# Cross network on one core: 32 rows of first-layer remainder weights copied on the chip, and VectorE's remainder copies ahead of three product pairs

## The chip, the cores and the metric

The kernel runs on one core of one Trainium2 chip. The metric is the device time of one execution in microseconds. Below, PE is TensorE (PEld its weight loads), DVE is VectorE, ACT is ScalarE, POOL is GpSimd and SP is SyncE. SP and ACT also issue DMA transfers, each from its own instruction queue.

## What is computed

```python
B, F, D, L = 4096, 26, 16, 6          # Din = F * D = 416
def reference(x0, ws, bs):            # x0 [4096, 416], ws [6, 416, 416], bs [6, 416], all bf16
    x = x0
    for l in range(ws.shape[0]):
        x = x0 * (x @ ws[l] + bs[l]) + x
    return x
```

Six layers; each is one matrix product over 416 features, a bias, a product with `x0` and a sum with the layer's input.

## The kernel before

The activations are held transposed on the chip: features on partitions, batch rows on columns. The 416 features are three full blocks of 128 (`XM`, index m for outputs, k for inputs) and a **remainder** of 32 (`XR`). The 4096 batch columns are two **halves** s = 0, 1 of 2048; a half is four **groups** g of 512 columns, and groups 0, 1 and 2, 3 form the two **pairs** h = 0, 1. The remainder of the four groups of a half lies on the four bands of 32 partitions of one tile, so its weights must be there four times: `WR` holds the 32 remainder rows of the weights on each band of 32 partitions. `XRd` holds `XR[0]` with the bands swapped by 64 partitions, and `WD` a 32-column slice of `WR`, each band in its own block.

The parts of the head that the change touches, by line:

- `load_x0t` (L76): one transposing DMA on SP for each group of a half, from `x0` in memory into `XM[0]`; eight in all. `load_xrem0` (L81): four DMAs on ACT that bring the remainder of half 0 into `xrig`. `load_xrem1` (L85): one DMA on SP that brings the remainder of half 1 into `xrem`; POOL rearranges it into `xrig` (L128).
- `load_wr0` (L88): one DMA on ACT that reads the 32 remainder rows of layer 0 four times, as a broadcast, into the 128 partitions of `WR`. `load_wr` (L91) does the later layers, four DMAs of 32 rows on SP. `fill_wd` (L125) copies from `WR` into `WD` on POOL.
- L106 is a small ACT instruction that makes the activation table load early.
- `first_layer(s)` runs layer 0 for one half. `full` (L206) multiplies the three full blocks of one group, `row` (L213) adds the remainder's part from `WR`, `mm_rem` (L185, L190) makes the remainder's output in `pr`. `x0_rem` transposes `xrig` on PE (L151) and copies the result on DVE into `XR[0]` once and into `XRd` in two parts (L154); for half 1 this stands inside `first_layer(0)`, after `mm_rem`, in the second bank of `pr`.
- `ew_main`: ACT evicts a PSUM tile with the bias (L159), DVE multiplies by `x0` (L160) and adds the layer's input (L161); these two are called a product pair below. `ew_rem` does the same for the remainder (L165, L166, L167).

PE in half 0 goes: the three `full` of group 0, the transposes of `xrig`, the three `full` of group 1, eight row matmuls (four calls of `row`, two matmuls each: three close the tiles of pair 0, one opens the first of pair 1), 18 matmuls of `full` for pair 1 (groups 2 and 3), four row matmuls, `mm_rem`, the transposes for half 1; then half 1 in the same manner. Four PSUM buffers of two banks go round among the tiles; the first tile of pair 1 in half 1, opened by the row matmuls, takes the buffer of half 0's `pr`, so it waits until ACT's L165 has read that.

Within an engine the order is made by a scheduler from the program and its own estimates; an instruction marked with `keep_in_program_order` is not moved past others so marked or ahead of its place. Each DMA signals one of eight completion semaphores, taken in turn; a DMA that takes a semaphore in use waits for the transfer before it.

Of the kernel before, what the change touches and what calls it, by code (L numbers as in the profile page):

```python
# [10 lines left out]
ALU = mybir.AluOpType  # L11
# [5 lines left out]
def kernel(  # L17
# [7 lines left out]
    nc = tc.nc  # L25
    B, D = x0.shape
    L = ws.shape[0]
    P = 128
    NK = 3
    R = D - NK * P  # L30
    assert R == 32 and B == 4096 and D == 416 and L >= 2
    NS = 2
    NG = 4
    CW = 512
# [18 lines left out]
    WR = const.tile([P, L, D], BF16)  # L53
# [11 lines left out]
    XM = [big.tile([P, NK, B], BF16, name=f"XM{i}") for i in range(3)]  # L65
    XR = [big.tile([P, NS * CW], BF16, name=f"XR{i}") for i in range(3)]

    def col0(s, g):
        return SW * s + CW * g
# [4 lines left out]
    def load_x0t(s, g):  # L74
        c0 = col0(s, g)
        nc.sync.dma_start_transpose(out=XM[0][:, :, c0:c0 + CW], in_=x0[c0:c0 + CW, 0:NK * P])  # L76
# [8 lines left out]
            nc.sync.dma_start(xrem[:], x0_v[:, 16:32, NK * P:D])  # L85

    def load_wr0():
        nc.scalar.dma_start(WR[:, 0, :], ws[0:1, NK * P:D, :].broadcast_to([NG, R, D]))  # L88

    def load_wr(eng, g, l0, l1):  # L90
        eng.dma_start(WR[32 * g:32 * g + 32, l0:l1, :], ws[l0:l1, NK * P:D, :].rearrange("l r n -> r l n"))  # L91
# [11 lines left out]
    load_x0t(0, 1)  # L103
    load_xrem0()
    load_wr0()
    nc.scalar.activation(dz[:, 1:2], dz[:, 0:1], ACT.Identity, bias=dz[:, 0:1], scale=1.0)  # L106
    for g in range(2, NG):
        load_x0t(0, g)
    load_x0t(1, 0)
# [39 lines left out]
    def x0_rem(s, tpr):  # L149
        for i in range(4):  # L150
            nc.tensor.transpose(tpr[:, 128 * i:128 * i + 128], xrig[:, s, i, :], ident[:])  # L151
        for dst, src in ((slice(0, P), slice(0, P)), (slice(64, P), slice(0, 64)), (slice(0, 64), slice(64, P))):
            to = XR[0] if dst == src else XRd
            nc.vector.tensor_copy(to[dst, CW * s:CW * s + CW], tpr[src])  # L154

    def ew_main(l, s, m, h, pt, cur, nxt):
        c0 = col0(s, 2 * h)
        t = tpool.tile([P, 2 * CW], BF16, name="t")
        nc.scalar.activation(t[:], pt[:].rearrange("p a b -> p (a b)"), ACT.Identity, bias=bM[:, m, l:l + 1], scale=1.0)  # L159
        nc.vector.tensor_tensor(out=t[:], in0=t[:], in1=XM[0][:, m, c0:c0 + 2 * CW], op=ALU.mult)  # L160
        nc.vector.tensor_tensor(out=nxt[:, m, c0:c0 + 2 * CW], in0=t[:], in1=cur[:, m, c0:c0 + 2 * CW], op=ALU.add)  # L161

    def ew_rem(l, s, pr, curR, nxtR):
        tr = tpool.tile([P, 2 * CW], BF16, name="t")
        nc.scalar.activation(tr[:, 0:CW], pr, ACT.Identity, bias=bR[:, l:l + 1], scale=1.0)  # L165
        nc.vector.tensor_tensor(out=tr[:, 0:CW], in0=tr[:, 0:CW], in1=XR[0][:, CW * s:CW * s + CW], op=ALU.mult)  # L166
        nc.vector.tensor_tensor(out=nxtR[:, CW * s:CW * s + CW], in0=tr[:, 0:CW], in1=curR[:, CW * s:CW * s + CW], op=ALU.add)  # L167
# [15 lines left out]
    def mm_rem(l, s, pr, cur, curR):  # L183
        for g in range(NG):
            nc.tensor.matmul(pr[32 * g:32 * g + 32, :], lhsT=WD[:, l, g, :], rhs=curR[:, CW * s:CW * s + CW],  # L185
                             start=True, stop=False, tile_position=(0, 32 * g))
        for k in range(NK):
            for g in range(NG):
                c0 = col0(s, g)
                nc.tensor.matmul(pr[32 * g:32 * g + 32, :], lhsT=WM[:, l, k, NK * P:D], rhs=cur[:, k, c0:c0 + CW],  # L190
                      start=False, stop=(k == NK - 1), tile_position=(0, 32 * g))
# [8 lines left out]
    def first_layer(s):  # L200
        cur, curR, nxt, nxtR = XM[0], XR[0], XM[1], XR[1]

        def full(pt, m, h, gl, after_row):
            c0 = col0(s, 2 * h + gl)
            for k in range(NK):
                nc.tensor.matmul(pt[:, gl, :], lhsT=WM[:, 0, k, 128 * m:128 * m + 128], rhs=cur[:, k, c0:c0 + CW],  # L206
                                 start=(k == 0 and not after_row), stop=(k == NK - 1 and after_row))

        def row(pt, m, h, opens):
            for gl in range(2):  # L210
                rg = 32 * ((2 * h + gl) ^ (2 if m == 1 else 0))
                src = XRd if m == 1 else curR
                nc.tensor.matmul(pt[:, gl, :], lhsT=WR[rg:rg + 32, 0, 128 * m:128 * m + 128],  # L213
                                 rhs=src[rg:rg + 32, CW * s:CW * s + CW],
                                 start=opens, stop=not opens, tile_position=(rg, 0))

        def ph(m):
            return psum.tile([P, 2, CW], FP32, tag="ps", name=f"ph{m}")

        pa = [ph(m) for m in range(NK)]  # L220
        if s == 0:
            for m in range(NK):
                full(pa[m], m, 0, 0, False)
            tp0 = psum.tile([P, CW], BF16, tag="ps", name="tpr")
            x0_rem(0, tp0[:])
            for m in range(NK):
                full(pa[m], m, 0, 1, False)
        else:
            for m in range(NK):
                for gl in range(2):  # L230
                    full(pa[m], m, 0, gl, False)
        pb = [ph(0)]
        row(pa[0], 0, 0, False)
        row(pb[0], 0, 1, True)
        row(pa[2], 2, 0, False)
        row(pa[1], 1, 0, False)
        for m in range(NK):
            ew_main(0, s, m, 0, pa[m], cur, nxt)
        for m in range(NK):
            if m:  # L240
                pb.append(ph(m))
            for gl in range(2):
                full(pb[m], m, 1, gl, m == 0)
        row(pb[1], 1, 1, False)
        row(pb[2], 2, 1, False)
        pr = psum.tile([P, 2, CW], FP32, tag="ps", name="pr")
        mm_rem(0, s, pr[:, 0, :], cur, curR)
        if s == 0:
            x0_rem(1, pr[:, 1, :].bitcast(BF16)[:, 0:CW])
        for m in range(NK):  # L250
            ew_main(0, s, m, 1, pb[m], cur, nxt)
        ew_rem(0, s, pr[:, 0, :], curR, nxtR)

    bias_setup()
# [1 line left out]
    for s in range(NS):  # L256
        first_layer(s)
# [15 lines left out]
    cur, curR = XM[1], XR[1]  # L273
    for l in range(1, LL):
        nxt, nxtR = XM[1 + (l % 2)], XR[1 + (l % 2)]
# [4 lines left out]
        def finish(t):  # L280
            s, m = t
            for h in range(2):
                ew_main(l, s, m, h, pts[t][h], cur, nxt)
            if feeds_last:
                xl_dmat(s, m, nxt)
# [19 lines left out]
        cur, curR = nxt, nxtR  # L305

    l = LL
# [97 lines left out]
```

## Time and profile before

Device times, 3 runs: median 131.31 us (131.15 to 131.46).

| what | value |
|---|---|
| profiled execution, its own time | 131.51 us |
| span, from first to last instruction | 129.7 us |
| PE busy | 123.4 us, 95% |
| DVE busy | 107.5 us, 83% |
| ACT busy | 85.7 us, 66% |
| POOL busy | 6.1 us, 5% |
| mean granted TensorE clock | 0.992 |
| DMA | 16.45 MB, 42185 packets |

Rows of a timeline are: start in us, length in us, engine, line, operation, written tile <- read tiles, count; in square brackets the engine's idle time before, and what ended it. SPq and ACTq are instructions of a queue, such as the issue of a DMA; the length of such a row is the issue's, and the landing comes later. Rows of groups end in busy time in us, mean ns of one, and idle time before with what ended it. Several instructions merged in a row overlap, since matmuls are pipelined.

### The profile page before, as it was taken

Reading aid. Unit: us, or ns where it says so; the run is one execution under the profiler, and the core shown is the slowest. Engines: PE = TensorE matmul, PEld = TensorE weight load, DVE = VectorE, ACT = ScalarE, POOL = GpSimd, SP = SyncE. Lnnn points to the kernel's source line nnn. Section 1 sums busy time; section 2 is a strip of 40 time slices with the busy share of each in tenths; the row PEclk is TensorE's granted clock in tenths of the full one; section 3 lists DMA queues with packets and bytes.
Section 4 is the critical chain, followed back from the end, with each engine's and each line's share of the span. In section 5 each row is a group of like instructions: output and inputs, shape, how many; then the busy total and the mean of one; then the engine's idle time right before and its main releaser. Section 6 shows DMA issues by size and latency. Waiting matters only on the chain.

```text
span 129.7 us, 3968 instructions
## 1 busy us (share of the span) xinstructions
PE 123.4 (95%) x1690; PEld 55.1 (42%) x1690; DVE 107.5 (83%) x197; ACT 85.7 (66%) x97; POOL 6.1 (5%) x17
## 2 busy tenths in 40 slices
PE   6999999999999999999999999999999999999960
PEld 2333343444444444444444444444444445445430
DVE  1022999999998898999898989898989899888992
ACT  0044865976849486849476849577848896569670
POOL 4002200800000000000000000000000000000000
PEclk9999999999999999999999999999999999999996
DMA  3999999999990000000000000000197989996754
GB/s 91 240 222 226 167 163 269 257 329 333 332 274 7 0 5 3 5 0 5 0 5 0 5 0 5 0 0 5 26 180 163 121 180 199 187 315 195 237 182 137
DMA packets 42185, 16.45 MB, mean 127 GB/s; under 512 B 30894, under 2 KB 42168, under 8 KB 42168
## 3 DMA queue, kind: packets, MB, share of 16 engines
q1 hardware_dynamic: 39368, 15.53, 54.3%
q10 hardware_dynamic: 2800, 0.67, 2.6%
q8 instruction: 13, 0.21, 0.7%
q14 instruction: 4, 0.03, 0.1%
HBM read 6.23 MB, written 3.41 MB: 74 GB/s over the span
## 4 chain that ended last, share of the span: by engine, by line
PE 73%; DVE 11%; DMA 8%; issue 3%; ACT 2%; DVEq 0%; ACTq 0%
PE pt L173 49%; PE py L319 8%; PE pt L179 5%; PE pr L190 4%; DMA WR<-in_ws_dram 4%; DMA XM<-in_x_dram 4%; DVE t L347 3%; PE ph L206 3%; DVE t L160 2%; DVE XM L161 2%; DVE o L336 2%; PE pr L185 2%; PE ph L213 1%; PE py L325 1%; ACT t L159 1%
## 5 line engine op out<-in xcount | busy, mean ns | idle before, releaser
L173 PE MATMUL pt<-XM,WM 128*32 128x512 bf16 x1152 | 65.2, 379 | 0.0
L159 ACT ACTIVATE t<-pt,bM 128x1024 bf16<-128x1024 f32 x48 | 49.6, 1115 | 18.3 <-PE pt L179 18.3
L160 DVE TENSOR_TENSOR t<-t,XM 128x1024 bf16<-128x1024 bf16 x60 | 41.4, 690 | 6.0 <-ACT t L159 6.0
L161 DVE TENSOR_TENSOR XM<-t,XM 128x1024 bf16<-128x1024 bf16 x60 | 41.8, 697 | 3.5
L173 PEld LDWEIGHTS <-WM 128*32 128x32 bf16 x1152 | 29.7, 97 | 33.8 <-issue 5.1
L346 ACT CAST t<-py 128x416 bf16<-128x416 f32 (+1 forms) x23 | 14.8, 642 | 4.8 <-PE py L319 2.1
L319 PE MATMUL py<-WM,XM 128*128 128x416 bf16 x96 | 17.7, 340 | 0.0
L206 PE MATMUL ph<-XM,WM 128*128 128x512 bf16 x72 | 16.5, 379 | 0.2 <-DMA XM<-in_x_dram 0.2
L159 ACT ACTIVATE t<-ph,bM 128x1024 bf16<-128x1024 f32 x12 | 12.5, 1115 | 4.9 <-PE ph L213 4.9
L319 PEld LDWEIGHTS <-XM 128*128 128x128 bf16 x96 | 9.0, 98 | 8.5 <-issue 1.4
L347 DVE TENSOR_TENSOR t<-t,X0rows 128x416 bf16<-128x416 bf16 (+1 forms) x23 | 10.4, 454 | 1.2 <-ACT t L346 1.2
L206 PEld LDWEIGHTS <-WM 128*128 128x128 bf16 x72 | 6.8, 98 | 8.6 <-issue 1.2
L336 DVE TENSOR_TENSOR o<-t,XLrows 128x416 bf16<-128x416 bf16 (+1 forms) x23 | 10.3, 451 | 0.0
L165 ACT ACTIVATE t<-pr,bR 128x512 bf16<-128x512 f32 x10 | 6.4, 684 | 5.0 <-DVE XRd L154 2.9
L190 PE MATMUL pr<-XM,WM 128*32 128x512 bf16 x120 | 8.2, 379 | 0.0
L179 PE MATMUL pt<-XR,WR 32*128 32x512 bf16 x96 | 7.3, 379 | 0.0
L106 ACT ACT_TABLE_LOAD x1 | 1.3, 1283 | 6.4 <-DMA XM<-in_x_dram 6.4
L135 PE MATMUL wps<-warm 128*128 128x512 bf16 (+1 forms) x11 | 4.1, 561 | 1.2 <-DVE warm L94 1.2
L167 DVE TENSOR_TENSOR XR<-t,XR 128x512 bf16<-128x512 bf16 x10 | 4.2, 424 | 0.7
L190 PEld LDWEIGHTS <-WM 128*32 128x32 bf16 x120 | 3.2, 97 | 3.0
L125 POOL COPY WD<-WR 32x32 bf16<-32x32 bf16 (+1 forms) x8 | 3.6, 454 | 16.0 <-DMA WR<-in_ws_dram 15.6
L166 DVE TENSOR_TENSOR t<-t,XR 128x512 bf16<-128x512 bf16 x10 | 4.2, 418 | 0.0
(37 smaller groups left out, 29.6 us busy)
## 6 DMA issues: line engine op xcount, KB each, us to landing
X0rows<-in_x_dram SPq DMA_DIRECT2D x4, 832.0 KB, 11.6
out_dram<-o SPq DMA_DIRECT2D x9, 208.0 KB, 2.6
WM<-in_ws_dram SPq DMA_DIRECT2D x5, 312.0 KB
out_dram<-o SPq DMA_DIRECT2D x13, 104.0 KB, 1.9
WR<-in_ws_dram SPq DMA_DIRECT2D x4, 130.0 KB, 4.2
WM<-in_ws_dram ACTq DMA_DIRECT2D x1, 312.0 KB
XM<-in_x_dram SPq DMA_TRANSPOSE x8, 5.7
xrig<-in_x_dram ACTq DMA_DIRECT2D x4, 32.0 KB, 4.3
```

The lines of the kernel that those rows point to most:

```text
L159: nc.scalar.activation(t[:], pt[:].rearrange("p a b -> p (a b)"), ACT.Identity, bias=bM[:, m, l:l + 1], scale=1.0)
L160: nc.vector.tensor_tensor(out=t[:], in0=t[:], in1=XM[0][:, m, c0:c0 + 2 * CW], op=ALU.mult)
L161: nc.vector.tensor_tensor(out=nxt[:, m, c0:c0 + 2 * CW], in0=t[:], in1=cur[:, m, c0:c0 + 2 * CW], op=ALU.add)
L165: nc.scalar.activation(tr[:, 0:CW], pr, ACT.Identity, bias=bR[:, l:l + 1], scale=1.0)
L173: nc.tensor.matmul(pts[g // 2][32 * q:32 * q + 32, g % 2, :], lhsT=WM[:, l, k, 128 * m + 32 * q:128 * m + 32 * q + 32], rhs=cur[:, k, c0:c ...
L179: nc.tensor.matmul(pts[g // 2][:, g % 2, :], lhsT=WR[32 * g:32 * g + 32, l, 128 * m:128 * m + 128], rhs=curR[32 * g:32 * g + 32, CW * s:CW ...
L190: nc.tensor.matmul(pr[32 * g:32 * g + 32, :], lhsT=WM[:, l, k, NK * P:D], rhs=cur[:, k, c0:c0 + CW], start=False, stop=(k == NK - 1), tile ...
L206: nc.tensor.matmul(pt[:, gl, :], lhsT=WM[:, 0, k, 128 * m:128 * m + 128], rhs=cur[:, k, c0:c0 + CW], start=(k == 0 and not after_row), sto ...
L319: nc.tensor.matmul(py[:, 0:D], lhsT=cur[:, k, q_cols(q, g)], rhs=WM[:, l, k, :], start=((not closes) and k == 0), stop=(closes and k == NK ...
L336: tc.keep_in_program_order(nc.vector.tensor_tensor(out=o, in0=t, in1=xl, op=ALU.add))
L346: nc.scalar.copy(tv, src)
L347: tc.keep_in_program_order(nc.vector.tensor_tensor(out=tv, in0=tv, in1=X0rows[:, b, :], op=ALU.mult))
```

## The change

The load of the first layer's remainder weights is now one DMA of the 32 rows into the first band of `WR`. It is issued on SP, behind the first two groups of `x0` (the scheduler puts it there too: on SP the list begins with two transposes, this load, then the other transposes). Three copies on the chip fill the other bands: two on ACT and one on POOL, behind L106 and ahead of `fill_wd`. And in half 0 the products of pair 1 carry the mark that keeps them in program order, so DVE makes the three copies of `x0_rem` for half 1 ahead of the fourth, fifth and sixth product pair; before, the scheduler had put them behind the fifth. PE's order is the same in both.

```diff
     def load_wr0():
-        nc.scalar.dma_start(WR[:, 0, :], ws[0:1, NK * P:D, :].broadcast_to([NG, R, D]))
+        nc.sync.dma_start(WR[0:R, 0, :], ws[0, NK * P:D, :])
...
     load_wr0()
     nc.scalar.activation(dz[:, 1:2], dz[:, 0:1], ACT.Identity, bias=dz[:, 0:1], scale=1.0)
+    for g in range(1, NG):
+        dst, src = WR[32 * g:32 * g + 32, 0, :], WR[0:R, 0, :]
+        if g < NG - 1:
+            nc.scalar.copy(dst, src)
+        else:
+            nc.gpsimd.tensor_copy(dst, src)
...
-    def ew_main(l, s, m, h, pt, cur, nxt):
+    def ew_main(l, s, m, h, pt, cur, nxt, pin=False):
...
-        nc.vector.tensor_tensor(out=t[:], in0=t[:], in1=XM[0][:, m, c0:c0 + 2 * CW], op=ALU.mult)
+        prod = nc.vector.tensor_tensor(out=t[:], in0=t[:], in1=XM[0][:, m, c0:c0 + 2 * CW], op=ALU.mult)
+        if pin:
+            tc.keep_in_program_order(prod)
...
         for m in range(NK):
-            ew_main(0, s, m, 1, pb[m], cur, nxt)
+            ew_main(0, s, m, 1, pb[m], cur, nxt, pin=(s == 0))
```

## The prediction

> **What bounds the kernel now.** I read the page first, then busy time by stage, then the chain of waits, and last the timelines of PE, DVE and SP over the first 35 us.
>
> ```profile
> 27.50:104.70 77.20, 77.20 (x1381) 34.56 (x1374) 69.99 (x115) 56.02 (x59) 0.00 (x0) 1.00 0.31 69
> ```
>
> A row of the stages: start and end, length, busy time and instructions of PE, PEld, DVE, ACT and POOL, granted clock, DMA share, GB/s. From 27.5 to 104.7 us PE is busy for all of 77.20 us at a granted clock of 1.00, so nothing edited before 27.5 us can shorten that stage; it can only start it earlier. The question is how many microseconds PE loses in the head. The chain of waits (start, length, what) shows two places.
>
> ```profile
> 0.74 5.01 DMA XM<-in_x_dram
> 5.76 5.23 DMA WR<-in_ws_dram
> 11.04 0.41 PE ph L213 x2
> ...
> 19.67 0.42 DVE XR L154
> 20.12 0.42 DVE XRd L154
> 20.56 0.44 DVE XRd L154
> 21.08 0.70 ACT t L165
> 21.82 0.60 PE ph L213 x6
> ```
>
> First, the remainder weights land at 5.76 + 5.23 = 10.99 and release the row matmuls. Second, ACT's eviction L165 stands behind VectorE's copies L154, and PE's rows behind L165, because `pr` gives back a PSUM buffer. PE's timeline gives the sizes.
>
> ```profile
> 8.83 2.10 PE L206 MATMUL ph<-XM,WM 128*128 128x512 bf16 x9
> 11.04 0.60 PE L213 MATMUL ph<-XR,WR 32*128 32x512 bf16 x6
> 11.59 4.15 PE L206 MATMUL ph<-XM,WM 128*128 128x512 bf16 x18
> 15.67 0.39 PE L213 MATMUL ph<-XRd,WR 32*128 32x512 bf16 x2
> 16.97 0.40 PE L151 MATMUL pr<-ident,xrig 128*128 128x128 bf16 x4
> 17.20 4.05 PE L206 MATMUL ph<-XM,WM 128*128 128x512 bf16 x18
> 21.19 0.39 PE L213 MATMUL ph<-XR,WR 32*128 32x512 bf16 x2
> 21.82 0.40 PE L213 MATMUL ph<-XR,WR 32*128 32x512 bf16 x4 [0.24 <-ACT t L165]
> 22.35 4.06 PE L206 MATMUL ph<-XM,WM 128*128 128x512 bf16 x18
> ```
>
> Undisturbed, 18 matmuls of L206 take 21.19 - 17.20 = 3.99 us up to the next rows. One step is (4.05 - 2.10)/9 = 0.217 us, so 9 of them take 3.99 - 9 x 0.217 = 2.04 us. Three losses follow:
> - the first rows could start at 8.83 + 2.04 = 10.87 and start at 11.04: **0.17 us**, waiting for WR;
> - the next 18 take 15.67 - 11.59 = 4.08 instead of 3.99: **0.09 us**. The only input first used there that can be late is the fourth x0 group, read from the fourth matmul on, so I put its landing at about 12.3 us (an estimate, 11.59 + 3 x 0.217 + 0.09);
> - the eight rows of the first half take 11.59 - 11.04 = 0.55 us, those of the second 22.35 - 21.19 = 1.16: **0.61 us**, waiting for L165. Only 0.24 is printed as idle; the rest is the pipe running dry.
>
> **The change, part by part.**
>
> *VectorE order (0.61 us).* In the compiled order nothing moves on PE; on DVE the three copies L154 stand after the third product pair instead of the fifth.
>
> ```profile
> 15.51 0.93 POOL L128 COPY xrig<-xrem 128x512 bf16<-128x512 bf16 x1 [3.39 <-DMA xrem<-in_x_dram]
> 16.01 0.98 DVE L161 TENSOR_TENSOR XM<-t,XM 128x1024 bf16<-128x1024 bf16 x1
> 31.44 0.41 DVE L167 TENSOR_TENSOR XR<-t,XR 128x512 bf16<-128x512 bf16 x1
> 34.42 0.22 PE pr L185 x4
> ```
>
> The third pair ends at 16.01 + 0.98 = 16.99, the transposes L151 that feed the copies at 16.97 + 0.40 = 17.37. With the first rows 0.17 earlier and PE 0.26 earlier, DVE has its pairs done at 16.82 and the transposes at 17.11. The copies wait some 0.3 to 0.4 us at the head of DVE's queue, with the fourth to sixth products behind them. They take 20.56 + 0.44 - 19.67 = 1.33 us and end near 18.5; L165 ends near 19.3, and PE's rows want it at 21.19 - 0.26 = 20.93. So the stall of 0.61 goes, with 1.6 us of cover. What is late next is DVE: it reaches the end of the first layer at 31.85 - 0.17 + 0.4, near 32.1. The first matmuls that need all of that are L185 of the second half, at 34.42, or 33.55 after the whole gain: 1.4 us of cover. Bounds: 0 gained if xrem comes so late that the copies gain nothing, 0.61 at best. I take 0.61.
>
> *WR on SP, 32 rows instead of 128 (0.17 us).* The load leaves ACT's queue, where it was issued after the first x0 group had landed, and stands on SP behind two transposes.
>
> ```profile
> 5.76 0.65 ACTq L88 DMA_DIRECT2D WR<-in_ws_dram  x1
> 2.17 2.69 SPq L76 DMA_TRANSPOSE XM<-in_x_dram  x1
> DMA to landing us min/median/max: 6.6/6.6/6.6
> 4.92 1.90 SPq L76 DMA_TRANSPOSE XM<-in_x_dram  x1
> 6.86 2.19 SPq L76 DMA_TRANSPOSE XM<-in_x_dram  x1
> 11.45 0.59 SPq L85 DMA_DIRECT2D xrem<-in_x_dram  x1
> DMA to landing us min/median/max: 3.9/3.9/3.9
> WR<-in_ws_dram SPq DMA_DIRECT2D x4, 130.0 KB, 4.2
> ```
>
> SP's second transpose ends its issue at 2.17 + 2.69 = 4.86, so WR is issued near 4.92. The landing rows are of that transpose (6.6, so 8.77), of xrem (3.9) and of the later WR loads (4.2). Bounds for its landing: 4.92 + 3.9 = 8.8 below, 10.99 as now above. I take 4.92 + 4.2 = 9.1, just behind the transpose ahead of it. Then two ACT copies and one POOL copy of 32x416, which the trace does not show. The nearest rows:
>
> ```profile
> L270 ACT COPY XLrows<-scrR 128x512 bf16<-128x512 bf16 x2 | 1.2, 625 | 0.7 <-DMA scrR<-XR 0.7
> L106 ACT ACTIVATE dz<-dz 128x1 f32<-128x1 f32 x1 | 0.3, 295 | 0.0
> L128 POOL COPY xrig<-xrem 128x512 bf16<-128x512 bf16 x1 | 0.9, 932 | 3.4 <-DMA xrem<-in_x_dram 3.4
> L125 POOL COPY WD<-WR 32x32 bf16<-32x32 bf16 x4 | 0.8, 204 | 9.2 <-DMA WR<-in_ws_dram 9.0
> ```
>
> ACT: between 295 and 625 ns; by width 0.295 + 415/511 x 0.330 = 0.56 us, two 1.13. POOL: between 204 and 932; by width 0.79. From 9.1 plus 0.1 for the semaphore ACT is done near 10.3, POOL near 10.0; PE wants them at 10.87. ACT has nothing else to do there (its first eviction follows the rows), and POOL's small copies L125 behind the new one are wanted only by L185, near 16 us. So the copies cost nothing while WR lands before 10.87 - 1.23 = 9.64; after that each microsecond costs one. I take the whole 0.17.
>
> *The transposes behind it (0.09 us).* Two effects pull apart. In the compiled order the third transpose now waits for the semaphore of the first, which lands at 5.75 (0.74 + 5.01 in the chain; ACT's old WR issue at 5.76 waited for the same), so its issue moves from 4.92 to about 5.8: **+0.88** for it and all that follows on SP, xrem included, plus the 26 KB. Against that stands a hole in the transfers:
>
> ```profile
> 8.30:9.60 1.30, 1.29 (x7) 0.59 (x7) 0.69 (x2) 0.00 (x0) 0.00 (x0) 1.00 1.26 295
> 9.60:10.70 1.10, 1.10 (x7) 0.39 (x4) 0.58 (x2) 0.00 (x0) 0.00 (x0) 1.00 1.29 101
> 10.70:12.00 1.30, 1.19 (x12) 0.33 (x11) 0.00 (x0) 0.53 (x1) 0.69 (x4) 1.00 1.28 287
> ```
>
> The last column is GB/s: 295, then 101, then 287, with the engines nominally busy throughout. The 1.1 us hole lies at the end of the WR transfer (landing 10.99), so I read it as transposes held up until WR's engines are through: at 290 GB/s it costs 1.1 x (290 - 101)/290 = 0.72 us. If it goes with the broadcast, the fourth group lands at 12.3 + 0.88 - 0.72 = 12.46 where every issue delay counts in full, and at 12.3 - 0.72 = 11.6 where the queue behind the second transpose covers the late issue. The second is nearer: its data still arrive until 8.77, 3 us after the new issue. PE wants that group at 12.34 - 0.09 - 0.17 = 12.08. I take it as in time: 0.09 gained; bounds 0.38 lost with the hole gone, and 1.1 lost with the hole left.
> The Trainium skill, DMA: Bandwidth & Descriptors, Rules for kernel authors, says that a leading zero-stride broadcast of c copies keeps a transfer on at most c engines. By it WR's broadcast of four copies sits on four and the 32-row form on sixteen, the hole goes and the sum below stands; without it rival 4 weighs more. The hole agrees with it but does not prove it.
>
> *Sum.* 0.61 + 0.17 + 0.09 = 0.87 us. The profiled execution took 131.51 us, 0.20 above the median 131.31; 130.64 on its scale, **130.44** against the median. PE's later stages have no gap to take it back, and the tail hangs on PE's end.
>
> **The rivals.**
> 1. *Only the VectorE order pays.* The fourth group still lands at 12.3, and the rows' 0.17 are spent waiting there: 131.31 - 0.61 = 130.70. For: 0.09 is lost there already. Against: the hole.
> 2. *The copies gate the rows.* WR lands 5.23 us after its issue, as now, at 10.15; the copies end at 11.38, 0.51 past 10.87: gain 0.36, 130.95. Against: it is a quarter of the bytes.
> 3. *The copies do not come forward.* xrem, last in the delayed line, holds POOL's copy and PE's transposes; the wait moves from L165 to L151, and only WR's part stays: 131.31 - 0.26 = 131.05. It decides from xrem 0.3 us later than now (POOL ends at 15.51 + 0.93 = 16.44, PE comes at 16.71) and has taken the 0.61 at 0.9 later.
> 4. *Slower: the third and fourth groups come late.* The hole is not the broadcast's, the issue delay counts in full: the fourth lands at 12.3 + 0.88 + 0.1 = 13.28 instead of 12.08, PE waits 1.2 us, and 131.31 - 0.87 + 1.2 = 131.64. It decides from a landing of 12.95. For: the transposes' issue is SP's only work there, back to back. Against: the rate outside the hole shows engines, not issue, as the limit.
>
> 5. *No change: SP's issue time passes on.* WR's own issue, 0.65 us on ACT, is added to SP's line, and the fourth group lands that much later, at 12.95; PE waits 0.87 us, and the time is 131.31. For: SP's issues follow each other without a pause (4.92 + 1.90 = 6.82, then 6.86). Against: the same rate. The Trainium skill, DMA: Bandwidth & Descriptors, Issuing engines are not separate DMA queues, says that a second issuing engine saves only the sequencer's issue time; the move gives that back. Whether it shows here the trace before cannot tell.
>
> **How the numbers follow.** Forecast 0.60, rival 1 0.12, rival 2 0.08, rival 3 0.08, rival 4 0.08, rival 5 0.04. The range runs from 130.2 (the forecast less the runs' scatter of 0.15 and the rounding of the steps) to 131.05, through rival 3; rivals 4 and 5, 0.12, stay outside. About 0.2%, 0.26 us, is what can be told from no change. Faster: forecast and rivals 1 and 2, 0.80; same: rivals 3 (at the edge) and 5, 0.12; slower: rival 4, 0.08.
>
> **What would show it.** The order step is right if L165 of the first half ends before 20 us and the eight rows of the second half take 0.55 us; wrong if L151 or L213 waits there. The WR step is right if WR lands near 9.1 and the first rows start near 10.87 with no wait on ACT or POOL. The transfer step is right if the 1.1 us hole is gone and the 18 matmuls after the first rows take 3.99 us. The forecast fails if PE waits for an x0 group, or if L185 of the next layer starts waiting on DVE.

## The result, and the profile after

The changed kernel takes 130.77 us (median of 13 runs, 130.49 to 131.15), the kernel before, run beside it, 131.28 (13 runs, 131.15 to 131.59): a ratio of 0.9965, 95% interval 0.9956 to 0.9974. The gain is 0.51 us, not the 0.87 of the forecast. The two profiled executions are further apart, 131.51 and 130.71, by 0.80; that contrast is taken up below.

PE's timeline of the changed kernel (the three blocks' matmuls are L214 now, the rows L221):

```profile
8.62 2.10 PE L214 MATMUL ph<-XM,WM 128*128 128x512 bf16 x9
10.66 0.60 PE L221 MATMUL ph<-XR,WR 32*128 32x512 bf16 x6
...
11.20 4.34 PE L214 MATMUL ph<-XM,WM 128*128 128x512 bf16 x18
15.47 0.39 PE L221 MATMUL ph<-XRd,WR 32*128 32x512 bf16 x2
...
21.00 0.60 PE L221 MATMUL ph<-XR,WR 32*128 32x512 bf16 x6
...
21.54 4.06 PE L214 MATMUL ph<-XM,WM 128*128 128x512 bf16 x18
```

The second half's rows take 21.54 - 21.00 = 0.54 us instead of 1.16: that stall is gone. The first rows begin at 10.66, directly behind the nine matmuls before them. But the 18 matmuls after them take 15.47 - 11.20 = 4.27 us, where 3.99 is the undisturbed time: PE loses 0.28 there, not 0. VectorE's timeline around the copies of the remainder:

```profile
17.21 0.42 DVE L160 COPY XR<-pr 128x512 bf16<-128x512 bf16 x1 [0.61 <-PE pr L157]
17.67 0.86 DVE L160 COPY XRd<-pr 64x512 bf16<-64x512 bf16 x2
```

ScalarE's, with the copies of `WR` and the eviction of `pr`:

```profile
8.82 1.10 ACT L110 COPY WR<-WR 32x416 bf16<-32x416 bf16 x2 [2.89 <-DMA WR<-in_ws_dram]
...
18.62 0.69 ACT L173 ACTIVATE t<-pr,bR 128x512 bf16<-128x512 f32 x1 [0.60 <-DVE XRd L160]
```

GpSimd's copy of `WR`:

```profile
8.94 0.53 POOL L112 COPY WR<-WR 32x416 bf16<-32x416 bf16 x1 [6.81 <-DMA WR<-in_ws_dram]
```

The copies of the remainder stand at 17.21 to 18.53, after 0.61 us at the head of DVE's queue, and the eviction of `pr` (L173) is through at 19.31, 1.7 us before PE wants it. WR has landed at 8.82, the copies on the chip end at 9.92 and 9.47, and PE comes at 10.66. The 0.28 us has its row in SP's timeline and in the chain of waits. SP first, then the chain:

```profile
4.77 0.57 SPq L88 DMA_DIRECT2D WR<-in_ws_dram  x1
5.61 5.17 SPq L76 DMA_TRANSPOSE XM<-in_x_dram  x3
```
```profile
0.74 4.86 DMA XM<-in_x_dram
5.61 1.44 SPq L76
7.10 5.00 DMA XM<-in_x_dram
12.14 3.40 PE ph L214 x15
...
126.04 0.29 DVEq L408
```

The first x0 group lands at 0.74 + 4.86 = 5.60; SP, which is done with the issue of `WR` at 4.77 + 0.57 = 5.34, issues the third transpose at 5.61, with the semaphore that this landing gives back (SP's waits put 0.3 us down to it); the fourth goes out at 7.10 and lands at 12.10, and only then do 15 of the 18 matmuls start. The last row stands behind DVE's last result, at 126.04. The stages, with GB/s in the last column:

```profile
8.30:9.60 1.30, 1.22 (x7) 0.60 (x7) 0.91 (x3) 0.75 (x2) 0.61 (x2) 1.00 1.12 237
9.60:10.70 1.10, 1.10 (x10) 0.34 (x11) 0.36 (x1) 0.32 (x1) 0.73 (x4) 1.00 1.24 267
10.70:12.00 1.30, 1.30 (x12) 0.38 (x12) 0.00 (x0) 0.91 (x1) 0.00 (x0) 1.00 1.04 138
...
27.50:104.70 77.20, 77.20 (x1374) 34.50 (x1362) 70.44 (x116) 56.01 (x59) 0.00 (x0) 1.00 0.33 72
```

The hole of 101 GB/s is filled (267), but the stages beside it are lower than before: 237 for 295 GB/s ahead of it, 138 for 287 behind it. From 8.30 to 12.00 us the change moves 781 KB (1.30 x 237 + 1.10 x 267 + 1.30 x 138) where the kernel before moves 868, at most 78 of them for the larger load of `WR` (104 KB instead of 26), so the x0 groups as a whole are no further on at 12 us. The middle of the kernel is as full as before: whatever the head gains is kept.

A second profiled execution of the kernel before, 131.35 us, is nearer to the median; it is called the usual one below. Its PE timeline, and two rows of its chain:

```profile
10.83 0.60 PE L213 MATMUL ph<-XR,WR 32*128 32x512 bf16 x6
...
11.37 4.29 PE L206 MATMUL ph<-XM,WM 128*128 128x512 bf16 x17
15.60 0.39 PE L213 MATMUL ph<-XRd,WR 32*128 32x512 bf16 x2
...
21.12 0.88 PE L213 MATMUL ph<-XR,WR 32*128 32x512 bf16 x6
...
22.14 0.82 PE L206 MATMUL ph<-XM,WM 128*128 128x512 bf16 x3
```
```profile
8.79 2.09 PE ph L206 x9
10.87 0.36 PE ph L213 x2
```

Here the first rows start at 10.83 and the chain goes to them from the nine matmuls before, not from WR; the 18 matmuls take 15.60 - 11.37 = 4.23 (0.24 lost; in the change, and with order only below, the chain puts such a loss down to the fourth x0 group), and the second half's eight rows take 22.14 - 21.12 = 1.02, a stall of 0.48 behind L165. In the execution that the prediction read, with its rows at 11.04, WR came some 0.2 us later than here. The two further profiles with the broadcast, those of order only below, have their first rows at 10.79 and 10.69, directly behind the nine matmuls as well.

### The profile page after: what moved, and what is told of

Its sections match the earlier page's. It is cut to its first block, busy times and chain, and to the rows that moved or that the text cites. A ratio compares the mean times of both kernels' runs of the same rounds, so it can differ in the third digit from the quotient of the medians.

```text
span 128.9 us, 3973 instructions
## 1 busy us (share of the span) xinstructions
PE 123.1 (96%) x1690; PEld 54.9 (43%) x1690; DVE 107.1 (83%) x197; ACT 86.9 (67%) x99; POOL 5.9 (5%) x18
## 4 chain that ended last, share of the span: by engine, by line
PE 80%; DMA 8%; DVE 5%; issue 2%; SPq 1%; ACT 1%; DVEq 0%
PE pt L181 49%; PE ph L214 9%; DMA XM<-in_x_dram 8%; PE py L327 8%; PE pt L187 5%; PE pr L198 5%; DVE t L355 3%; DVE o L344 2%; PE pr L193 2%; SPq L76 1%; PE py L333 1%; PE ph L221 1%; PE py L336 1%; ACT t L354 1%; PE pr L157 0%
## 5 line engine op out<-in xcount | busy, mean ns | idle before, releaser
L165 ACT ACTIVATE t<-pt,bM 128x1024 bf16<-128x1024 f32 x48 | 49.6, 1115 | 18.3 <-PE pt L187 18.3
L214 PE MATMUL ph<-XM,WM 128*128 128x512 bf16 x72 | 16.5, 379 | 0.1
L165 ACT ACTIVATE t<-ph,bM 128x1024 bf16<-128x1024 f32 x12 | 12.5, 1114 | 4.4 <-PE ph L221 4.4
L214 PEld LDWEIGHTS <-WM 128*128 128x128 bf16 x72 | 6.8, 98 | 8.6 <-issue 1.3
L173 ACT ACTIVATE t<-pr,bR 128x512 bf16<-128x512 f32 x10 | 6.4, 684 | 2.7 <-PE pr L198 2.1
L175 DVE TENSOR_TENSOR XR<-t,XR 128x512 bf16<-128x512 bf16 x10 | 4.2, 423 | 0.7
## 6 DMA issues: line engine op xcount, KB each, us to landing
X0rows<-in_x_dram SPq DMA_DIRECT2D x4, 832.0 KB, 11.6
```

## The experiments

The kernel before was run beside them in three sets, each on a chip of its own: 131.27 us (21 runs) for the first, 131.28 (26) for the second, 131.18 (23) for the third. Line numbers shift from kernel to kernel: the matmuls of the three blocks are L206, L208, L214, L216 or L218, the rows L213, L215, L221, L223 or L225, the eviction of `pr` L165, L173 or L175.

**Each part alone.** "Order only" adds to the kernel before nothing but the mark on the products of pair 1 in half 0; "WR only" is the change without the mark. Against the kernel before, order only is:

```diff
-    def ew_main(l, s, m, h, pt, cur, nxt):
+    def ew_main(l, s, m, h, pt, cur, nxt, pin=False):
...
-        nc.vector.tensor_tensor(out=t[:], in0=t[:], in1=XM[0][:, m, c0:c0 + 2 * CW], op=ALU.mult)
+        prod = nc.vector.tensor_tensor(out=t[:], in0=t[:], in1=XM[0][:, m, c0:c0 + 2 * CW], op=ALU.mult)
+        if pin:
+            tc.keep_in_program_order(prod)
...
-            ew_main(0, s, m, 1, pb[m], cur, nxt)
+            ew_main(0, s, m, 1, pb[m], cur, nxt, pin=(s == 0))
```

Against the changed kernel, WR only is:

```diff
-            ew_main(0, s, m, 1, pb[m], cur, nxt, pin=(s == 0))
+            ew_main(0, s, m, 1, pb[m], cur, nxt)
```

> Only VectorE's order is changed; the broadcast load of WR on ACT stays. Theory A (the profile of before hides the x0 groups behind the late L165, the profile of after ends on the fourth x0 group): the second half's eight rows take 0.55 us instead of 1.16, the rows of the first half still start near 11.04 on WR and the fourth group still lands near 12.3, so the gain is 0.6 us at most, about 130.7, and most of the gain of the whole change is this. Theory B (the three terms of the prediction add up): 131.28 - 0.61 = 130.67, and the whole change then beats it by 0.26.

> The 32-row load on SP and the three copies, without the change of VectorE's order. Theory A: the first rows start near 10.66 instead of 11.04, the whole VectorE chain up to L165 moves forward by as much, and a wait of 0.3 us for the fourth x0 group is absorbed in front of L165: gain 0.2 to 0.4 us, 130.9 to 131.1, and the second half's rows take 0.7 to 1.0 us. Theory B: the gain is 0.26, 131.02, and the wait for the fourth group would be paid on top.

Order only: 131.01 us (10 runs, 130.81 to 131.15), ratio 0.9978 [0.9969, 0.9987]. WR only: 131.54 (12 runs, 131.32 to 132.12), 1.0024 [1.0013, 1.0036], slower than before. Both missed what was expected: either theory had order only at 130.67 to 130.7, and WR only between 130.9 and 131.1. PE's timeline with the order alone, its stage from 9.6 to 10.7 us, its chain, and one row of PE's timeline with WR only:

```profile
21.09 0.60 PE L215 MATMUL ph<-XR,WR 32*128 32x512 bf16 x6
...
21.63 1.25 PE L208 MATMUL ph<-XM,WM 128*128 128x512 bf16 x5
```
```profile
9.60:10.70 1.10, 1.10 (x6) 0.39 (x4) 0.49 (x2) 0.00 (x0) 0.00 (x0) 1.00 0.63 108
```
```profile
6.92 5.28 DMA XM<-in_x_dram
12.24 3.40 PE ph L208 x15
```
```profile
22.18 4.06 PE L214 MATMUL ph<-XM,WM 128*128 128x512 bf16 x18
```

With the order alone the rows take 0.54 as in the change, the hole is there as before (108 GB/s), and the fourth x0 group lands at 12.20. So the order removes the stall by itself, and with the 32-row load that group comes only 0.10 earlier (12.10): its issue is 0.18 later (7.10 against 6.92), and it lands 5.00 us after it instead of 5.28. With WR only PE's matmuls go on at 22.18, no earlier than the usual 22.14. There the fourth transpose goes out later still, at 7.21, and the 18 matmuls take 15.40 - 11.40 = 4.00 all the same, so in that execution the group was in time: the late issue does not cost the same in every run.

**The 32-row load elsewhere.** The changed kernel with the load on ACT's queue, where the broadcast was, and with the load on POOL's queue (there with POOL's copies, `fill_wd` and the one of `xrig` among them, marked to stay in program order). On ACT, and then on POOL:

```diff
-        nc.sync.dma_start(WR[0:R, 0, :], ws[0, NK * P:D, :])
+        nc.scalar.dma_start(WR[0:R, 0, :], ws[0, NK * P:D, :])
```
```diff
-        nc.sync.dma_start(WR[0:R, 0, :], ws[0, NK * P:D, :])
+        nc.gpsimd.dma_start(WR[0:R, 0, :], ws[0, NK * P:D, :])
...
-            nc.gpsimd.tensor_copy(dst, src)
+            tc.keep_in_program_order(nc.gpsimd.tensor_copy(dst, src))
...
```

> The whole change, but the 32-row load is issued on ACT, where the broadcast was. SP's third transpose then has a free semaphore and is issued near 4.9 instead of 5.6. If the fourth group is late in the changed kernel because of that wait and of WR's issue on SP, it lands 0.5 us or more earlier, at 11.2 to 11.7, and PE does not wait for it; but WR, issued near 5.7, lands at 9.2 to 9.9, so the copies end between 10.4 and 11.1 and the first rows wait 0 to 0.4 us. 130.4 to 130.7. If the late group has another cause (the transfers themselves), it lands near 12.1 as before and the time is that of the whole change, 130.8, or worse.

> The whole change, but the 32-row load is issued on POOL, on a queue and semaphore of its own, so SP has neither WR's issue nor the wait of the third transpose; POOL's copies are held in program order. Theory A with SP's line as the cause: WR lands before 8 us, the copies are long done at 10.66, the fourth group lands at 11.2 to 11.7 and PE does not wait for it: 130.3 to 130.5, 0.3 us below the whole change. If SP's line is not the cause: fourth group near 12.1, 130.8.

On ACT: 130.72 us (6 runs, 130.62 to 130.86), 0.9953 [0.9941, 0.9965]. On POOL: 130.64 (5 runs, 130.59 to 130.72), 0.9949 [0.9937, 0.9961]. Both lie above what was expected, 130.4 to 130.7 and 130.3 to 130.5, by 0.02 and 0.14. The stage with the load on ACT, and ACT's copies:

```profile
9.60:10.70 1.10, 1.10 (x7) 0.41 (x5) 0.62 (x2) 0.75 (x2) 0.60 (x2) 1.00 1.27 286
```
```profile
9.93 1.10 ACT L110 COPY WR<-WR 32x416 bf16<-32x416 bf16 x2 [1.99 <-DMA WR<-in_ws_dram]
```

With the load on POOL, PE's timeline, SP's row of the fourth transpose, and how long that transpose took to land:

```profile
11.30 4.06 PE L216 MATMUL ph<-XM,WM 128*128 128x512 bf16 x18
15.29 0.39 PE L223 MATMUL ph<-XRd,WR 32*128 32x512 bf16 x2
```
```profile
6.92 2.04 SPq L76 DMA_TRANSPOSE XM<-in_x_dram  x1
```
```profile
DMA to landing us min/median/max: 4.8/4.8/4.8
```

Between order only and the load on ACT nothing differs but the form of the load (and the copies it needs), and the stage goes from 108 to 286 GB/s: in this pair the hole goes with the broadcast. The Trainium skill, DMA: Bandwidth & Descriptors, Rules for kernel authors, confines a leading broadcast of four copies to at most four engines. The drop fits that, but does not prove it: no view counts the engines of one transfer, and the DMA share in the hole (the last column but one) runs from 0.49 to 1.29 over the four profiles with the broadcast. With the load on POOL SP's transposes go out as in order only (fourth at 6.92), the group lands at 6.92 + 4.8 = 11.7, PE wants it near 11.95 (11.30 + 3 x 0.217), and the 18 matmuls take 15.29 - 11.30 = 3.99. With the load on ACT `WR` lands later, the copies end at 9.93 + 1.10 = 11.03 and hold the first rows up by some 0.17 us (0.71 for the eight instead of 0.54): rival 2's mechanism, in that kernel and not in the change. For the x0 groups, the load on POOL shows what the prediction had put down for the change itself.

**The same without the order.** The load on POOL without the mark on the products; against the load on POOL:

```diff
-            ew_main(0, s, m, 1, pb[m], cur, nxt, pin=(s == 0))
+            ew_main(0, s, m, 1, pb[m], cur, nxt, pin=False)
```

> WR on POOL's queue and the copies, as in e4, but VectorE's order of before. Theory A: what the weights and the x0 groups gain ahead of the second half is lost again in front of L165, whose time hangs on the VectorE chain alone; that chain starts with the first rows, which gain 0 to 0.1 us: 131.2 to 131.3, and the second half's rows take 1.1 us or more. Theory B (the terms add up): 131.27 - 0.26 = 131.0.

131.58 us (9 runs, 131.54 to 131.97), 1.0029 [1.0016, 1.0042], against the 131.2 to 131.3 expected. Its chain, and then the same stretch of the chain of the kernel before (its second profile):

```profile
15.03 1.03 DVE t L168
...
16.68 0.70 DVE t L168
...
20.87 0.70 ACT t L175
...
22.21 0.97 PE ph L216 x4
```
```profile
15.15 0.61 DVE t L160
...
16.70 0.69 DVE t L160
...
20.87 0.69 ACT t L165
...
22.21 0.97 PE ph L206 x4
```

PE's rows after the 18 matmuls begin at 15.24 here and at 15.60 in the kernel before, 0.36 apart; from 16.7 on both chains are the same to 0.02 us, through VectorE's products and copies to the eviction L165 and PE. That chain begins at the first rows, not at the fourth group: from the first rows to VectorE's fourth product it takes 5.87 us in both profiles of the kernel before (11.04 to 16.91, 10.83 to 16.70) and with WR only (10.86 to 16.73). So as long as VectorE's order stands as it was, nothing that an earlier x0 group gains comes out behind L165, and a wait for x0 there costs nothing either; a late WR does come out, the 0.21 us between the two profiles of the kernel before. Here the first rows are 0.13 us earlier than in the second of them (10.70), but the third product takes 0.42 us longer in the chain (1.03 for 0.61) and the addition behind it only 0.29 less (0.69 for 0.98), and the lead is gone. POOL's copy of `xrig` runs beside that product (14.78 to 15.49); that it is the cause was not tried.

**The semaphore.** The changed kernel with the load of the biases (`bsb`) on POOL's queue, which lets the third transpose go without waiting for the first.

```diff
-    nc.scalar.dma_start(bsb[:], bs[:, :])
+    nc.gpsimd.dma_start(bsb[:], bs[:, :])
```

> The whole change with WR on SP, but the small load of the biases moved from ACT to POOL: one semaphore of the eight becomes free, so SP's third transpose no longer waits for the first group's landing (5.6) and is issued right behind WR's issue, near 5.35. If the wait for the semaphore is what delays the fourth group, it lands 0.25 us earlier, at 11.8 to 11.9, PE waits hardly at all, and the time comes near e4's 130.64; if WR's own issue on SP is what delays it, little changes and the time stays near 130.75.

> The changed kernel once more, beside the others of this call. Theory A: about 130.75; the wait of PE for the fourth x0 group is there again and is what differs from run to run, 0.1 to 0.7 us; the first rows do not wait for WR.

> The kernel before once more, for a second profile. Theory A: the first profile, 131.51, caught a late landing of WR; in a run near the median 131.27 the first rows start 0 to 0.1 us after PE could have started them, so the 0.17 us of the prediction are hardly there, while the second half's rows still take about 1.1 to 1.2 us behind L165. If the first rows again wait 0.17 us and more, the 0.17 is a steady loss and its missing gain has another cause.

131.28 us (12 runs, 130.94 to 133.02), 1.0007 [0.9985, 1.0029], beside the changed kernel at 131.17 (12 runs, 130.77 to 131.59), 0.999 [0.9976, 1.0004]. It settles nothing: in its profiled execution (132.82 us) the biases came late and PE waited for them, so it has a fault of its own, and the third transpose, now without a wait, still goes out only at 5.77, because the load's issue ahead of it is later too (5.14 to 5.71). On this chip the change gained 0.11 us, which the interval does not tell from nothing. In its profile here the fourth group held PE up until 12.24, and the eighth took a further 0.2 us in the second half.

**SP's line alone.** Last, on one chip, the change, order only and the load on POOL once more, and beside them the load on POOL with a second load of 32 rows, which nobody reads, put on SP between the second and the third transpose. It adds that transfer to the work.

```diff
+    spare = const.tile([R, D], BF16)
...
+        nc.sync.dma_start(spare[:], ws[1, NK * P:D, :])
```

> The changed kernel once more, beside the three kernels below on one chip. It has given 130.77 (130.49 to 131.15) and 131.17 (130.77 to 131.59) on two chips. Theory A (the load in SP's line costs it: its issue, then a wait for the first x0 group's semaphore, bring the third transpose from 4.9 to 5.6 us and the fourth x0 group to 12.1 or later): a median between 130.7 and 131.2 with lows and highs 0.6 us apart or more, and in the profile PE waits 0.2 to 0.5 us for XM at about 12.2. Theory B (the difference of the chips, not the line): the same median as the kernel with the load on POOL's queue, within 0.1 us.

> The changed kernel with the 32-row load on POOL's queue, once more. Theory A: 130.6 to 130.7, lows and highs less than 0.3 us apart, no wait of PE for XM between 11.3 and 15.3 us, and below the changed kernel by 0.1 to 0.5 us. Theory B: within 0.1 us of the changed kernel on the same chip.

> VectorE's order alone, the load as a broadcast on ACT, once more. Theory A: about 131.0, 0.3 below the kernel before and 0.3 to 0.4 above the load on POOL's queue, because the broadcast's hole (about 100 GB/s in the stage from 9.6 to 10.7 us) keeps the fourth x0 group at 12.2 or later. Theory B (the load's form and place are worth nothing, all of the gain is the order): the same as the kernel with the load on POOL's queue, within 0.1 us.

> The kernel with the load on POOL's queue, and on SP, between the second and the third transpose, a second load of 32 rows into a tile that nothing reads (it adds 26 KB of transfer). Its data are nobody's, so only SP's line is as in the change. Theory A: the third transpose is issued at 5.6 instead of 4.9 us, the fourth x0 group lands near 12.1, PE waits 0.2 to 0.5 us for XM at about 12.2, and the time is that of the changed kernel on this chip within 0.2 us, 0.1 to 0.5 above the kernel without the dummy. Theory C (what counts is when and from where the remainder weights themselves are loaded, not SP's line): the time of the kernel without the dummy, within 0.1 us, and no wait of PE for XM.

| kernel | median us (runs, range) | ratio to before |
|---|---|---|
| the change | 130.81 (7, 130.45 to 131.06) | 0.9965 [0.9952, 0.9978] |
| load on POOL | 130.70 (5, 130.65 to 130.88) | 0.9965 [0.9953, 0.9976] |
| order only | 130.91 (10, 130.81 to 131.02) | 0.9977 [0.9968, 0.9986] |
| load on POOL, spare load on SP | 130.93 (12, 130.59 to 131.37) | 0.998 [0.9968, 0.9992] |

SP's timeline of the kernel with the spare load, its chain, and one row of its PE timeline:

```profile
4.72 0.57 SPq L90 DMA_DIRECT2D spare<-in_ws_dram  x1
5.83 5.47 SPq L77 DMA_TRANSPOSE XM<-in_x_dram  x3
```
```profile
0.74 5.07 DMA XM<-in_x_dram
5.83 1.41 SPq L77
7.29 5.36 DMA XM<-in_x_dram
12.69 3.40 PE ph L218 x15
```
```profile
12.69 3.40 PE L218 MATMUL ph<-XM,WM 128*128 128x512 bf16 x15 [0.53 <-DMA XM<-in_x_dram]
```

The spare load brings back the late group: the third transpose at 5.83, the fourth at 7.29 landing at 12.65, PE waiting 0.53 us, the median 0.23 us higher, and a spread of 0.78 us where the kernel without it has 0.23. The profiled execution is the slowest of its 12; the fastest, 130.59 and 130.60, are as fast as without the spare load. The remainder weights are in place long before the rows (the copies end at 7.45), so theory C falls: what holds the group up comes with a load in SP's line. The issue takes 0.57 us in both; the pause behind it, up to the landing of the first group, is 0.27 us in the change (5.34 to 5.61) and 0.54 here (5.29 to 5.83, the landing at 5.81). Issue, semaphore and the 26 KB of the transfer itself were not taken apart further. For the change against the load on POOL the third set is weaker than theory A asked: the medians are 0.11 apart, the intervals the same. What stands is the spread, 0.61 against 0.23, and the change's fastest runs (130.45) are as good as any. That its slower ones are those in which x0 comes late fits the profiles, but is not shown: no fast run of it was profiled. Order only stands 0.21 above the load on POOL, where theory A had 0.3 to 0.4 and theory B at most 0.1.

## Why the prediction was right, and where its size was off

One table carries the argument: where PE goes on behind the second half's rows, where DVE's last result is out, and the profiled execution's own time.

| kernel | PE goes on | DVE done | own time | after DVE |
|---|---|---|---|---|
| before | 22.35 | 126.85 | 131.51 | 4.66 |
| before, second profile | 22.14 | 126.64 | 131.35 | 4.71 |
| WR only | 22.18 | 126.68 | 131.52 | 4.84 |
| load on POOL, no order | 22.14 | 126.65 | 131.54 | 4.89 |
| order only | 21.63 | 126.13 | 130.99 | 4.86 |
| order only, third set | 21.52 | 126.03 | 130.91 | 4.88 |
| the change | 21.54 | 126.04 | 130.71 | 4.67 |
| the change, second set | 21.64 | 126.34 | 131.02 | 4.68 |
| the change, third set | 21.89 | 126.40 | 131.06 | 4.66 |
| load on ACT | 21.67 | 126.17 | 130.86 | 4.69 |
| load on POOL | 21.35 | 125.85 | 130.62 | 4.77 |
| load on POOL, third set | 21.34 | 125.84 | 130.66 | 4.82 |
| spare load on SP | 22.08 | 126.59 | 131.37 | 4.78 |

The second column less the first is 104.50 or 104.51 in every row but one (the change in the second set, where the eighth x0 group took 0.2 more). So the head alone decides when DVE is done, as the prediction had it from the stage of 77.20 us. The last column is what lies behind the kernel's last result. It lies between 4.66 and 4.89, and the profiles of one program agree in it to 0.05; it makes the medians of order only and WR only look some 0.2 us worse than their heads are. It arises behind the issue of the last store, which comes 0.31 us after DVE's last result in the change and 0.32 with order only (126.35 and 126.45). Its cause stays open.

Point by point:

- *VectorE's order* was right, and so was its cover: copies after the third pair, L173 through at 19.31 (forecast 19.3), eight rows in 0.54 us (0.55). DVE is through with the first layer at 31.69, not near 32.1 as forecast (31.85 before), and the matmuls that need it (L193 of the second half, now at 33.43) follow without a wait. In the two profiled executions it is worth 1.16 - 0.54 = 0.62 for the 0.61 taken; against the usual kernel before, 1.02 - 0.54 = 0.48. By DVE's last result order only gains 126.64 - 126.13 = 0.51, and 0.61 in its second profile (126.03).
- *The WR step* was right in every time: landing 8.8 (forecast 9.1), ACT's copies 0.55 each (0.56), POOL's 0.53 (0.79), no wait on them. Its gain is not: "the first rows could start at 8.83 + 2.04 = 10.87 and start at 11.04: **0.17 us**" was the lateness of WR in one execution: in the three other profiles with the broadcast the rows start directly behind the nine matmuls, at 10.83, 10.79 and 10.69. The same lateness is most of the 0.20 us by which that execution stood above the median. "130.64 on its scale, 130.44 against the median" therefore took it off twice. Without that the sum gives 131.31 - 0.61 - 0.09 = 130.61.
- *The transfer step* failed: "I take it as in time: 0.09 gained". The hole of that stage did go (267 GB/s), with less moved in the stages beside it, and the fourth group landed at 12.10 instead of near 11.6, and PE waited for it; 0.28 lost instead of 0.09 gained in the change's first profile. The issue delay of 0.88 was itself smaller (fourth transpose 7.10 for 6.86, since the third's issue took 1.44 us for 1.90), but for the missing hole the landing was quicker only by 5.00 against 5.28. On POOL's queue, with the fourth transpose at 6.92, it took 4.8; the spare load on SP took that gain away again, so the load in SP's line does this. And the wait that it found was not new: the kernel before loses 0.24 there too, but behind L165 that cost nothing. Once the order step has removed L165, PE hangs on x0's landing instead.
- *The rivals.* Rival 1, only the VectorE order pays and the rows' gain is spent waiting for the fourth group, is what happened, and its 130.70 is nearest to the 130.77. By DVE's last result the change (126.04, 126.34, 126.40) is no earlier than order only (126.13, 126.03). The last of the three is the slowest of its 7 runs, but the medians say the same: with each program's last column taken off they give 126.10, 126.49 and 126.15 for the change, 126.15 and 126.03 for order only (an estimate from the table). Rivals 2 and 3 fall: no copy of `WR` gated a row, and xrem was in time (POOL's copy ends at 16.05, PE comes at 16.78). Rival 4's price of 0.88 did not come, nor rival 5's sum, though rival 5's reason is the right one: SP's line passes its time on. The Trainium skill, DMA: Bandwidth & Descriptors, Issuing engines are not separate DMA queues, calls the issue time saved by another engine usually small beside the transfer; here the place in the line was worth 126.04 - 125.85 = 0.19 us to 126.40 - 125.84 = 0.56 of DVE's last result in the profiled executions, and 0.13 and 0.11 in the medians.

In short, the forecast of faster was right by the order alone; the other two terms, 0.26 together, came to nothing in the change. The prediction's own sign of failure, "if PE waits for an x0 group", did appear. That 130.77 lies between 130.2 and 131.05 is owed to rivals 1 to 3, for which the range was left wide, and in that sense to luck: the sum of 0.87 was too large by 0.36. Nor is the gain steady: 0.51, 0.11 and 0.37 us in the three comparisons with the kernel before. The version that pays most is the load on POOL's queue: 130.64 and 130.70 in two sets, with spreads of 0.13 and 0.23.

## What to carry to other kernels

Profile the kernel before twice: a wait seen in one execution may be that execution's own, and if the profile stands above the median, a loss read in it must not be taken off the median as well. Where a stall is fed by a chain on another engine, every input that does not feed that chain has slack; removing the stall lets that slack go, and the next input in the line (here a transposed group behind one more small load) becomes the limit. A small load put into the queue that issues the inputs can make those behind it late, by its issue or by the semaphore it takes (here the fourth group at 12.10 instead of 11.7); a queue with nothing urgent behind it is the better place for it.

## What the runs showed of the hardware

- While a transfer that is read as a broadcast over four bands is under way beside the transposes, the core moves less: 98 to 122 GB/s in the stage from 9.6 to 10.7 us in the four profiles with it, 286 with 32 rows from the same queue. Without a broadcast, but with the third transpose late, the stage stood at 267, 240 and 177 in the three profiles of the change, at 226 with WR only and at 152 with the spare load; why was not tried.
- PE ran at about half speed after a pause in the head, once. In the kernel with the biases on POOL's queue (PE's timeline, then its stage):

```profile
6.67 0.24 PE L149 MATMUL pb<-ident,bsb 6*128 6x6 bf16 x3 [1.03 <-DMA bsb<-in_bs_dram]
...
6.96 3.76 PE L214 MATMUL ph<-XM,WM 128*128 128x512 bf16 x9
```
```profile
6.60:8.30 1.70, 1.62 (x11) 0.77 (x12) 0.25 (x2) 0.00 (x0) 0.00 (x0) 1.00 1.25 204
```

PE idles 1.03 us and then takes 3.76 us for nine matmuls that take 2.12 in the change, although the clock column of the stage reads 1.00. A pause alone does not settle it: with the load on ACT PE idles 0.83 us directly ahead of its nine matmuls, and they take 2.10. The Trainium skill, TensorE: Matmul & The Clock Gate, Part 1: The HAM clock gate, gives 426.7 ns as the start-to-start of 512 columns on a cold array and 215.7 on a warm one; 3.76 over nine, about 0.42, is near the first. Why this execution was slow is not shown.
